# Strided attention and a SoLU layer on one core: a rebuilt first stage, and the mean taken off the activations instead of the weights

## The chip, the cores and the metric

The kernel runs on one core of one Trainium2 chip. The core has five engines with their own in-order instruction streams: TensorE (PE), VectorE (DVE), ScalarE (ACT), GpSimd (POOL) and SyncE (SP, which here only issues DMAs). The metric is the device time of one execution in microseconds; the figure shown is the median of three runs.

## What is computed

Eight batches, eight heads, 576 positions, head width 64. Four heads attend locally (the last 32 positions), four attend to every position with the same residue modulo 32. The 4608 x 512 result goes through a feed-forward layer with a softmax-weighted linear unit and a layer norm:

```python
scores = scale * np.matmul(q, k.transpose(0, 1, 3, 2))
mask_local = (rel >= 0) & (rel < 32)
mask_strided = (rel >= 0) & (pos[None, :] % 32 == pos[:, None] % 32)
attn = softmax(where(mask, scores, -1e9)); x = attn @ v      # to (4608, 512)
h = x @ w_in                                                  # 512 x 1024
sm = np.exp(h - h_max) / (np.sum(np.exp(h - h_max)) + 1e-09)
solu = h * sm
ln = (solu - mean(solu)) / np.sqrt(var(solu) + 1e-06) * g_ln
out = ln @ w_out                                              # 1024 x 512
```

q, k, v are float32. w_in and w_out come as 64-bit floats, 4 MB each, and are turned into float32 on the chip from their two 32-bit words. Products are kept near float32 by splitting each factor into a float16 part (hi) and a float16 remainder (lo) and adding three products.

## The kernel before

Every instruction group is a step with an engine, an estimated duration and a key (`Plan.add`). `Plan.order` walks a small model of the engines and emits the steps in the order in which the model would start them, the lowest key first among those that are ready. The order on each engine is therefore fixed when the program is written out; what the model gets wrong shows as waiting.

Attention runs in 40 units, five per batch (`UNITS`): two strided ones (54 queries x 54 keys in 6 and 5 blocks per head pair), then three local ones (64 x 96, 3 blocks). In `unit`, PE writes mask plus scores to `s_ps` (L347, L352), DVE takes the maximum and subtracts it (L358, L359), ACT takes the exp (L361), DVE the sums and reciprocals (L362, L366, L367), POOL multiplies (L370), ACT writes the hi part (L376) and DVE the lo part (L377) of p, a DMA transposes p to pt (L379), PE multiplies with v to `x_ps` (L400), and ACT and DVE write xhi and xlo (L416, L417) into a ring that the feed-forward part reads.

Per batch, `v_scale` squares v on ACT (L289), sums over partitions by f32 matmuls with a matrix of ones (`pow2_scale`, L254) and makes a power-of-two scale; `v_split` makes v's hi and lo parts (L307, L308). For the strided heads, two blocks of v lie in the two halves of the partitions, and four SBUF-to-SBUF DMAs a batch (L323) copy them to `vd`, so that one product takes p's hi and lo parts stacked in the partitions.

The feed-forward part has 36 tiles of 128 tokens (`ff`). G1: 24 matmuls of 512 columns to `h_ps` (L458 to L460). Then DVE's maximum (L465, L466), ACT's exp (L467), DVE's u = h times e with its sum (L469), the mean (L472), ACT's sum of (u - mean) squared (L473), POOL's norm (L477 to L487), c = u times r as hi on ACT (L490) and lo on DVE (L491), a DMA transpose to ct (L494). G2: 24 matmuls with w_out to `o_ps` (L498 to L500), and ACT scales and stores (L506, L507).

The weights are prepared once. `decode` reads a 512-column piece (L522), ACT widens one word (L525), DVE shifts and ors the other (L528, L529). `prep_w` squares w_in on ACT (L541), makes its scale, writes whi on ACT (L549) and gets wlo as a product on PE (L553, L555) that ACT copies (L557). `prep_o` does the same for w_out, and centres it: u's mean is not subtracted from u, but the weighted column mean is subtracted from w_out, with `gmat` (L567, L574) for the means and `split_o`'s `gdiag` and `ones` times `mt` (L590, L591) on PE, from which ACT and DVE write ohi and olo (L594, L595). Tile 0's G2 needs all of it.

Loads go out on SP in the order of the plan; SP waits when too many are outstanding.

Of the kernel before, what the change touches and what calls it, by code (L numbers as in the profile page):

```python
# [7 lines left out]
F32 = mybir.dt.float32  # L8
# [44 lines left out]
VK = [-25.0, *(5.0 * b - 8.0 for b in range(1, B))]  # L53
# [3 lines left out]
LF = [-62, -61, -59.55, -59.5, -59.45]  # L57
LW = [-60.0 + 0.1 * i for i in range(8)] + [-48.0 + 0.1 * i for i in range(8)]


class Plan:
# [12 lines left out]
    def add(self, eng, dur, fn, key, r=(), w=(), lock=None):  # L74
        n = len(self.steps)
        deps = set()
# [13 lines left out]
        self.steps.append((eng, dur, fn, key, deps, lock))  # L90

    def order(self):
# [15 lines left out]
        while len(out) < len(steps):  # L108
# [12 lines left out]
            if e == "sp":  # L121
                dma_free = max(dma_free, now + 0.55) + dur
                free[e] = max(now + 0.55, dma_free - self.DMA_AHEAD)
                end = dma_free + self.DMA_LATENCY
            else:
                if steps[n][5]:
                    now = max(now, locked["pool" if e == "dve" else "dve"])
                    locked[e] = now + dur
                free[e] = end = now + dur
# [10 lines left out]
def attn_solu_kernel(ctx: ExitStack, tc: tile.TileContext, qloc, qstr, kloc, kstr, vloc, vstr, w_in, w_out, g, masks, out):  # L140
# [13 lines left out]
    rooms = buf("room", [P, 1024], I32, n=4)  # L154
    (junk,) = buf("junk", [P, 6 * 4 * D], BF16)

    vr_sb = buf("vrl", [P, NCL * 4 * D]) + buf("vrs", [P, 6 * 4 * D])
    v_sb = buf("vl", [P, 2, NCL * 4 * D], F16) + buf("vs", [P, 2, 6 * 4 * D], F16)
    (ve_sb,) = buf("ve", [KL, 2, NCL * 4 * D], F16)

    (vd_sb,) = buf("vd", [P, 2, 6, 2, 4 * D], F16)
    vm_sb = buf("vm", [P, 4], n=2)
    vsc_sb = buf("vsc", [P, 5], n=4)
# [12 lines left out]
    e_sb = buf("e", [P, DF], n=2)  # L176
    u_sb = buf("u", [P, DF], n=2)
# [3 lines left out]
    st_sb = buf("st", [P, 16], n=4)  # L181
    (gmat,) = buf("gmat", [P, 8, P])
    (gdiag,) = buf("gdiag", [P, 8, P])
    (minus,) = buf("minus", [P, P], F16)
    (mt_sb,) = buf("mt", [P, DM])
    (nhalf,) = buf("nhalf", [P, 1])
    (ones,) = buf("ones", [P, P])
    (w16,) = buf("w16", [P, 4, 2, DF], F16)

    (obuf,) = buf("obuf", [P, 8, DM])  # L190
    o16 = obuf.bitcast(F16).rearrange("p c (a f) -> p c a f", a=2)
    whi, wlo = w16[:, :, 0, :], w16[:, :, 1, :]
    ohi, olo = o16[:, :, 0, :], o16[:, :, 1, :]
    (w_sc,) = buf("w_sc", [P, 8])
    (o_sc,) = buf("o_sc", [P, 16])
    (g_sb,) = buf("g", [P, 8])

# [8 lines left out]
    def init():  # L206
        nc.vector.memset(nhalf, -0.5)

    add("dve", 0.2, init, -9, w=["nhalf"])
# [9 lines left out]
    def load_masks(key):  # L219
        add("sp", 0.6, lambda: nc.sync.dma_start(mask_sb, masks), key, w=["mask_raw"])  # L220
        add("dve", 1.5, masks_bf16, key, r=["mask_raw"], w=["mask"])
# [8 lines left out]

    add("pool", 1.6, lambda: nc.gpsimd.memset(vd_sb[D:P, 1].bitcast(F32), 0.0), -9, w=["vz"])
# [14 lines left out]
    def pow2_scale(dst, parts, key, r, w, room, top=14, mul=1.0, square=None):  # L246
# [5 lines left out]
        def total():  # L252
            for i, part in enumerate(parts):
                nc.tensor.matmul(tot, ones, part, start=(i == 0), stop=(i == len(parts) - 1))  # L254

        add("pe", 0.2 * len(parts), total, key, r=["ones", *r], w=[T])
# [5 lines left out]
        def fn():  # L262
# [4 lines left out]
            if square:  # L267
                nc.vector.tensor_scalar(dst[:, 2:3], dst[:, 1:2], dst[:, 1:2], square, op0=ALU.mult, op1=ALU.mult)

        add("dve", 0.2, root, key, r=[T], w=[(w, "root")])  # L270
        add("dve", 0.5, fn, key, r=[(w, "root")], w=[w])


    def load_qk(b, half, key):
        w = 2 * (S, SP)[half]
        k0 = 0 if half else KPAD
        add("sp", 1.65, lambda: nc.sync.dma_start(q_raw[half][:, 0:w], (qloc, qstr)[half][b]), key, w=[("q", half)])
# [416 lines left out]
```

## Time and profile before

| | us |
|---|---|
| median of three runs | 572.67 |
| lowest and highest run | 567.52, 572.97 |
| span of the profiled execution, first to last instruction | 566.9 |
| PE, DVE, ACT, POOL busy in it | 505.7, 355.9, 301.8, 156.7 |

The profile gives no time of its own for the profiled execution beyond its span; that span is 0.6 us below the lowest run. Matmuls overlap on PE, so the sum of their durations in a group is more than the time that they took; the start-to-start distance is what counts. In a row of a group, "busy, mean ns" is followed by the idle time of the engine just before those instructions and by what ended it. In a row of the waits stand the total, the number of times and the longest. In a table of stretches each engine has its busy time and number of instructions, then come TensorE's granted clock (1.00 is full), the mean busy share of the 16 DMA engines and what they moved in GB/s.

### The profile page before, as it was taken

How to read it: one execution, taken by the hardware profiler on the slowest of the kernel's cores; microseconds unless marked ns; L12 is line 12 of the kernel's file. 1: busy time of each engine (PE TensorE's matmuls, PEld its weight loads, DVE VectorE, ACT ScalarE, POOL GpSimd, SP SyncE). 2: the span in 40 equal slices, each digit the busy share in tenths (PEclk: the TensorE clock that was granted, in tenths of full speed). 3: DMA queues.
4: the chain of work that ended last, by engine and by line, in shares of the span. 5: the costliest groups of instructions: out<-in, count | busy, mean ns of one | idle time of the engine just before them, and what ended most of it. 6: DMA issues, size and time to landing. Idle time of an engine off the chain costs nothing.

```text
span 566.9 us, 11879 instructions
## 1 busy us (share of the span) xinstructions
PE 505.7 (89%) x4864; PEld 256.9 (45%) x4864; DVE 355.9 (63%) x633; ACT 301.8 (53%) x446; POOL 156.7 (28%) x309
## 2 busy tenths in 40 slices
PE   0348998999798999899999999999989999999986
PEld 0233444345453555455454554555545554444432
DVE  3596367867466775677766776877656777343430
ACT  3765824685256553755674556555744644345350
POOL 2320002433132342334331332322323323113130
PEclk9999978899999999999999999999999999999999
DMA  8999149629992999599938996899679635533332
GB/s 312 413 258 272 35 120 227 140 59 247 190 250 56 225 217 237 127 175 236 254 86 122 271 221 138 198 206 240 162 137 180 139 80 111 87 84 84 77 91 74
DMA packets 171158, 96.90 MB, mean 171 GB/s; under 512 B 138208, under 2 KB 157280, under 8 KB 171104
## 3 DMA queue, kind: packets, MB, share of 16 engines
q1 hardware_dynamic: 165920, 86.71, 70.8%
q10 hardware_dynamic: 5184, 9.44, 5.1%
q8 instruction: 38, 0.62, 0.5%
q14 instruction: 16, 0.13, 0.1%
HBM read 39.24 MB, written 9.44 MB: 86 GB/s over the span
## 4 chain that ended last, share of the span: by engine, by line
PE 72%; DVE 10%; DMA 9%; ACT 5%; issue 2%; POOL 1%; ACTq 0%; SPq 0%; DVEq 0%
PE h_ps L458 10%; PE h_ps L459 9%; PE h_ps L460 9%; PE o_ps L498 9%; PE o_ps L499 9%; PE o_ps L500 9%; PE x_ps L400 4%; PE s_ps L352 4%; DMA pt<-p 3%; DMA ct<-c 2%; DVE u L469 2%; DMA vrl<-vloc 2%; ACT e L467 2%; PE h_ps L553 2%; PE s_ps L347 1%
## 5 line engine op out<-in xcount | busy, mean ns | idle before, releaser
L458 PE MATMUL h_ps<-w,xhi 128*128 128x512 f16 x280 | 108.5, 388 | 10.5 <-DVE u L469 7.6
L459 PE MATMUL h_ps<-w,xhi 128*128 128x512 f16 x280 | 108.2, 386 | 0.0
L460 PE MATMUL h_ps<-w,xlo 128*128 128x512 f16 x280 | 107.7, 385 | 0.0
L498 PE MATMUL o_ps<-obuf,ct 128*128 128x512 f16 x272 | 103.4, 380 | 1.0 <-DMA ct<-c 0.8
L499 PE MATMUL o_ps<-obuf,ct 128*128 128x512 f16 x272 | 103.3, 380 | 0.0
L500 PE MATMUL o_ps<-obuf,ct 128*128 128x512 f16 x272 | 103.2, 379 | 0.0
L370 POOL TENSOR_TENSOR t<-t,m 128x576 f32<-128x576 f32 (+2 forms) x40 | 47.4, 1184 | 126.9 <-DVE m L367 101.1
L467 ACT ACTIVATE e<-h_ps,st,vsc 128x1024 f32<-128x1024 f32 x31 | 37.2, 1201 | 64.8 <-DVE st L466 49.4
L465 DVE TENSOR_REDUCE st<-h_ps 128x1 f32<-128x1024 f32 x35 | 42.6, 1218 | 41.9 <-PE h_ps L460 41.9
L477 POOL TENSOR_SCALAR st<-st 128x1 f32<-128x1 f32 x36 | 11.4, 316 | 208.3 <-DVE st L472 198.8
L469 DVE SCALAR_TENSOR_TENSOR u<-h_ps,e 128x1024 f32<-128x1024 f32 x35 | 42.8, 1222 | 29.1 <-ACT e L467 17.7
L473 ACT ACTIVATE e<-u,st 128x1024 f32<-128x1024 f32 x36 | 41.3, 1147 | 35.3 <-DVE st L472 32.1
L491 DVE SCALAR_TENSOR_TENSOR c<-u,st,c 128x1024 f16<-128x1024 f32 x36 | 47.0, 1304 | 14.6 <-ACT c L490 14.6
L417 DVE TENSOR_TENSOR xlo<-x_ps,xhi 128x384 f16<-128x384 f32 (+2 forms) x40 | 25.6, 641 | 40.4 <-ACT xhi L416 40.3
L490 ACT ACTIVATE c<-u,st 128x1024 f16<-128x1024 f32 x36 | 41.2, 1145 | 16.8 <-POOL st L487 16.0
L459 PEld LDWEIGHTS <-xhi 128*128 128x128 f16 x288 | 28.5, 99 | 40.2 <-issue 12.9
L498 PEld LDWEIGHTS <-ct 128*128 128x128 f16 x288 | 28.2, 98 | 39.4 <-DMA ct<-c 5.5
L458 PEld LDWEIGHTS <-xhi 128*128 128x128 f16 x288 | 28.8, 100 | 35.4 <-issue 5.9
L460 PEld LDWEIGHTS <-xlo 128*128 128x128 f16 x288 | 28.6, 99 | 35.4 <-issue 2.5
L500 PEld LDWEIGHTS <-ct 128*128 128x128 f16 x288 | 28.2, 98 | 34.2 <-issue 0.3
L499 PEld LDWEIGHTS <-ct 128*128 128x128 f16 x288 | 28.2, 98 | 32.3
L352 PE MATMUL s_ps<-k,q 64*54 64x54 f32 (+1 forms) x1280 | 41.8, 274 | 0.0
(143 smaller groups left out, 766.2 us busy)
## 6 DMA issues: line engine op xcount, KB each, us to landing
out<-ob ACTq DMA_DIRECT2D x36, 256.0 KB, 3.1
vrs<-vstr SPq DMA_DIRECT2D x8, 768.0 KB, 5.8
vd<-vs SPq DMA_DIRECT2D x16, 384.0 KB, 7.5
vrl<-vloc SPq DMA_DIRECT2D x8, 640.0 KB, 5.7
q<-qstr SPq DMA_DIRECT2D x8, 594.0 KB, 4.9
k<-kstr SPq DMA_DIRECT2D x8, 594.0 KB, 6.5
q<-qloc SPq DMA_DIRECT2D x8, 576.0 KB, 5.2
k<-kloc SPq DMA_DIRECT2D x8, 576.0 KB, 6.8
```

Of the source, the lines that this page charges most:

```text
L352: nc.tensor.matmul(s_ps[row : row + nq, pair, i * nk : (i + 1) * nk], q_raw[half][hs, q0 : q0 + (nq - 1) * nqb + 1 : nqb], k_raw[half][hs, ...
L370: add("pool", nx * nk / 500 + 0.1, lambda: nc.gpsimd.tensor_tensor(tv, tv, sm.unsqueeze(2).broadcast_to([P, nx, nk]), op=ALU.mult), key + ...
L458: nc.tensor.matmul(hv[:, i], xhi[:, cc, tok], whi[:, cc, cols], start=(cc == 0), stop=False)
L459: nc.tensor.matmul(hv[:, i], xhi[:, cc, tok], wlo[:, cc, cols], start=False, stop=False)
L460: nc.tensor.matmul(hv[:, i], xlo[:, cc, tok], whi[:, cc, cols], start=False, stop=(cc == 3))
L465: add("dve", 1.21, lambda: nc.vector.tensor_reduce(nm, hv, axis=AX.XY, op=ALU.max, negate=True), key + 0.2, r=HH, w=[(ST, "nm")])
L467: add("act", 1.3, lambda: nc.scalar.activation(ev, hv, AF.Exp, bias=nm, scale=hs, accum_out=z), key + 0.25, r=[*HH, (ST, "nm"), *SC], w=[E ...
L469: add("dve", 1.3, lambda: nc.vector.scalar_tensor_tensor(uv, hv, 1.0, ev, op0=ALU.mult, op1=ALU.mult, accum_out=us), key + 0.3, r=[*HH, E] ...
L491: add("dve", 1.35, lambda: nc.vector.scalar_tensor_tensor(c[:, 1], u, r, c[:, 0], op0=ALU.mult, op1=ALU.subtract), key + 0.45, r=[U, (ST, ...
L498: nc.tensor.matmul(o, ct[:, cc, :], ohi[:, cc, :], start=(cc == 0), stop=False)
L499: nc.tensor.matmul(o, ct[:, cc, :], olo[:, cc, :], start=False, stop=False)
L500: nc.tensor.matmul(o, ct[:, 8 + cc, :], ohi[:, cc, :], start=False, stop=(cc == 7))
```

## The change

- **Strided v.** `vd` and its four copies a batch are gone. `load_v` reads the strided v twice from HBM, once to partitions 0 to 63 and once to 64 to 127, in two transfers of 64 partitions; `vrs` and `vs` are twice as wide (3072 columns), and the split covers both places. The products read `vs` where they read `vd`.
- **Sums of squares.** For w_in and for batch 0's v, PE forms the Gram matrix of the upper 16 bits of the floats, and one DVE pass sums its diagonal. For later batches ACT squares in three passes instead of two. `pow2_scale` sums the parts on DVE and over partitions with one bf16 matmul.
- **Decoding** works on 1024 columns a piece: four pieces of 1 MB for each weight. w_in's lo part is made on PE for two row blocks as before, on DVE for the other two.
- **The mean** is subtracted from u: c = (u - mean), hi on ACT as an activation with a bias, lo on DVE; r is left to the store's factor f. u is scaled by a power of two `ia` made from the row's largest value. The squares come after c, and POOL's five small passes make f from them. w_out is scaled by g and a power of two, with no product on PE.
- **lo of p** goes to POOL for batch 0's units (`POOL_LO`).
- **Order.** `Plan.ahead` gives every step that the first tile's G1, and then its G2, depends on a key by its longest chain. The planner's model of DMAs counts outstanding pushes; durations are changed throughout. w_out's loads are held in the plan until the transposes of units 1 and 2 are issued, later loads until certain transposes.

```diff
+    def ahead(self, target, base):
+        tail = {target: 0.0}
+        for n in range(target, -1, -1):
+            if n not in tail:
+                continue
+            for d in self.steps[n][4]:
+                tail[d] = max(tail.get(d, 0.0), tail[n] + self.steps[n][1] + self.HOP)
+        for n, t in tail.items():
+            s = list(self.steps[n])
+            lands = s[6][2] + s[6][3] if s[6] else 0.0
+            s[3] = min(s[3], base - t - s[1] - lands)
...
+    def gram(dst, pieces, key, w, room, scrap):
+        acc, A = room
+        for i, (x, r) in enumerate(pieces):
+            def products(i=i, x=x):
+                y = x.bitcast(BF16).rearrange("p (f t) -> p f t", t=2)
+                n = x.shape[1]
+                for f in range(0, n, P):
+                    z = y[:, f : f + P, 1]
+                    nc.tensor.matmul(acc, z, z, start=(i == 0 and f == 0), stop=(i == len(pieces) - 1 and f == n - P))
...
+        add("dve", 0.35, lambda: nc.vector.scalar_tensor_tensor(scrap, acc, 2.0 ** (-2 * SQ), unit_sb, op0=ALU.mult, op1=ALU.mult, accum_out=dst),
...
+        add("pe", 0.15, lambda: nc.tensor.matmul(tot, ones, one, start=True, stop=True), key, r=["ones", *r], w=[T])
...
+        for i in range(2):
+            def twice(i=i):
+                nc.sync.dma_start(vr_sb[1][i * D : i * D + D].rearrange("p (y f) -> p y f", y=2), vstr[b].rearrange("(y p) f -> p y f", y=2))
...
-            moves = [(1.5, vd_sb[0:D, :, :, y], vn[y * D : y * D + D]) for y in range(2)]
-            moves += [(0.8, vd_sb[D:P, 0, :, y], vn[y * D : y * D + D, 0]) for y in range(2)]
+            moves = ()
...
+        if b < POOL_LO:
+            add("pool", nx * nk / 510 + 0.02, lambda: nc.gpsimd.tensor_tensor(lo, tv, hi, op=ALU.subtract), key + 0.45, r=[T, PB], w=[PB])
...
+        add("dve", 0.2, lambda: nc.vector.tensor_tensor(st[:, 0:3], low.broadcast_to([P, 3]), sc[:, 0:3], op=ALU.mult), key + 0.2,
...
+        def span():
+            nc.vector.tensor_scalar(near, up, floor, down, op0=ALU.max, op1=ALU.max)
+            nc.vector.tensor_scalar(ia.bitcast(I32), near.bitcast(I32), 0x7FFFFFFF, 0x7F800000, op0=ALU.bitwise_xor, op1=ALU.bitwise_and)
...
-        add("act", 1.2, lambda: nc.scalar.mul(c[:, 0], u, r), key + 0.4, r=[U, (ST, "r")], w=[(C, 0)])
+        add("act", 1.2, lambda: nc.scalar.activation(c[:, 0], u, AF.Identity, bias=mean, scale=1.0), key + 0.35, r=[U, (ST, "mean")], w=[(C, 0)])
+        add("dve", 1.28, lambda: nc.vector.scalar_tensor_tensor(c[:, 1], u, mean, c[:, 0], op0=ALU.add, op1=ALU.subtract), key + 0.4,
+        add("act", 1.24, lambda: nc.scalar.activation(junk[:, 0:DF], u, AF.Square, bias=mean, scale=1.0, accum_out=sq), key + 0.42,
...
-                nc.tensor.matmul(x, gdiag[:, cc], obuf[:, cc], start=True, stop=False)
-                nc.tensor.matmul(x, ones[0:1], mt_sb[0:1], start=False, stop=True)
+            add("act", 0.68, lambda cc=cc, go=go: nc.scalar.mul(ohi[:, cc], o32[:, cc], go), key, r=[("od", cc), "go"], w=[("oh", cc), *past])
+                add("dve", 0.7, lambda cc=cc, go=go: nc.vector.scalar_tensor_tensor(olo[:, cc], o32[:, cc], go, ohi[:, cc], op0=ALU.mult, op1=ALU.subtract), key,
...
+    for target, base in ((second[1], -200.0), (second[0], -200.0), (first[1], -400.0), (first[0], -400.0)):
+        plan.ahead(target, base)
```

More of the change, by code (lines that the diff above doesn't have):

```diff
@@ new lines, in v_scale, with square @@
+        parts = () if b == 0 else ((vr_sb[0], 0), (vr_sb[1][:, 0 : 6 * 4 * D], 1), (vr_sb[1][:, 6 * 4 * D :], 1))
+        for i, (x, a) in enumerate(parts):
+            def square(i=i, x=x):
+                nc.scalar.activation(junk[:, 0 : x.shape[1]], x, AF.Square, scale=2.0**-SQ, accum_out=vm[:, i : i + 1])
+            add("act", (1.36, 1.58)[a], square, key, r=VR[a], w=["junk", ("vm", b % 2, i)])
+        pow2_scale(sc, vm[:, 0 : 3 if b else 1], vs1_sb[b % 2], key, [("vm", b % 2, i) for i in range(3 if b else 1)], ("vsc", b % 4),
+                   (o_ps[:, P : P + 1], "o") if b == 0 else (s_ps[:, 1, 511:512], ("s", 1)), 8, 1.0 / P_SCALE)
@@ L303, in v_split @@
+        add("dve", 0.36, hscale, key + 0.5, r=[("vsc", b % 4), "w_sc", "consts"], w=[("hsc", b % 4)])
     def v_split(b, a, key):
@@ L557, in prep_w @@
+                add("pe", 1.4, rest, key, r=["wdiag", "minus", ("wh", cc), *ST[cc]], w=[X])
                 add("act", 0.62, lambda cc=cc, x=x, cols=cols: nc.scalar.copy(wlo[:, cc, cols], x), key, r=[X], w=[("w", cc, i)])
     def prep_o(key):
-        for cc in range(8):
-            decode(obuf[:, cc], w_out[cc * P : (cc + 1) * P, :], key, ("od", cc), O_ROOMS[cc], 8 + cc)
-            add("act", 0.6, lambda cc=cc: nc.scalar.activation(ob_sb[cc % 2][:, 0 : DM // 2].bitcast(BF16), obuf[:, cc], AF.Square,
-                                                               scale=2.0**-SQ, accum_out=o_sc[:, 8 + cc : 9 + cc]), key,
-                r=[("od", cc)], w=[("om", cc), ("ob", cc % 2)])
@@ L566, in gains @@
-        def gains():
-            nc.gpsimd.tensor_scalar(gmat, g_sb.unsqueeze(2).broadcast_to([P, 8, P]), -1.0 / DF, None, op0=ALU.mult)
-        add("pool", 2.3, gains, key - 5, r=["g"], w=["gmat"])
-        add("pool", 2.3, lambda: nc.gpsimd.tensor_tensor(gdiag, unit_sb.unsqueeze(1).broadcast_to([P, 8, P]), g_sb.unsqueeze(2).broadcast_to([P, 8, P]), op=ALU.mult),
-            key - 5, r=["g", "unit"], w=["gdiag"])
-        for cc in range(8):
-            add("pe", 0.87, lambda cc=cc: nc.tensor.matmul(o_ps, gmat[:, cc], obuf[:, cc], start=(cc == 0), stop=(cc == 7)), key,
-                r=["gmat", ("od", cc)], w=["o"])
@@ L577, in comb @@
[L577 to L583 removed]
+        add("pool", 0.3, lambda: nc.gpsimd.tensor_tensor(gg_sb[:, 0], g_sb, g_sb, op=ALU.mult), key, r=["g"], w=["gg"])
@@ new lines, in prep_o @@
+        for i in range(4):
+            dst, D2 = o32[:, 2 * i : 2 * i + 2], [("od", 2 * i), ("od", 2 * i + 1)]
+            decode(dst, w_out[2 * i * P : (2 * i + 2) * P].rearrange("(c p) (f t) -> p c f t", c=2, t=2), key, D2, ROOMS[(i + 2) % 4], 4 + i, [turned[AFTER_O[i]]])
+            for cc in (2 * i, 2 * i + 1):
+                add("act", 0.8, lambda cc=cc: nc.scalar.activation(ob_sb[cc % 2][:, 0 : DM // 2].bitcast(BF16), o32[:, cc], AF.Square,
+                                                                   scale=2.0**-SQ, accum_out=o_sc[:, 4 + cc : 5 + cc]), key,
+                    r=[("od", cc)], w=[("om", cc), ("ob", cc % 2)])
```

335 lines of the change are left out of this document (181 added, 154 removed).

## The prediction

> **What bounds the kernel now.** I read the page first (span, busy shares, 40 slices), then a table of stretches, the timeline of PE, PE's waits, and the chain of waits at the end.
>
> ```profile
> span 566.9 us, 11879 instructions
> ...
> core 0: us, PE busy (x) PEld busy (x) DVE busy (x) ACT busy (x) POOL busy (x), PEclk, DMA share, GB/s
> 0.00:10.00 10.00, 0.00 (x0) 0.00 (x0) 1.67 (x8) 1.88 (x2) 4.07 (x15) 1.00 0.80 272
> 10.00:20.00 10.00, 0.30 (x2) 0.30 (x2) 5.24 (x10) 6.42 (x12) 0.00 (x0) 1.00 1.02 414
> 0.00:66.40 66.40, 30.26 (x328) 17.48 (x329) 39.13 (x78) 41.59 (x71) 13.38 (x21) 1.00 0.92 275
> 66.40:123.30 56.90, 53.21 (x401) 24.45 (x399) 38.95 (x76) 29.07 (x45) 13.79 (x24) 0.88 0.59 135
> 100.00:540.00 440.00, 424.16 (x4176) 215.51 (x4171) 289.83 (x501) 240.52 (x347) 134.88 (x271) 0.99 0.78 163
> ```
>
> From 100 to 540 us PE is busy 424.16 of 440: that stretch is bound by PE, and 15.8 us of waits are all that any other engine could give there. What is slack lies in front. Until 66.4 us PE works 30.26 and idles 36.1; and of the 53.21 that it works from 66.4 to 123.3, part is preparation. The timeline of PE names the milestones:
>
> ```profile
> 19.70 0.58 PE L254 MATMUL s_ps<-vm,ones 128*128 128x1 f32 x2 [19.70 <-ACT junk L289]
> 22.65 0.49 PE L347 MATMUL s_ps<-mk_str,unit 64*64 64x324 bf16 x4 [0.75 <-DVE vsc L260]
> 66.47 0.38 PE L458 MATMUL h_ps<-w,xhi 128*128 128x512 f16 x1
> 66.69 0.38 PE L459 MATMUL h_ps<-w,xhi 128*128 128x512 f16 x1
> 123.32 0.39 PE L498 MATMUL o_ps<-obuf,ct 128*128 128x512 f16 x1
> ```
>
> The scores of unit 0 (L347) need only q, k and the masks, and the masks were there at 6.7 us (below); they start at 22.65 because PE, in order, first waits for ACT's squares of v. The first product for a token tile ("G1", L458) starts at 66.47, the first output product ("G2", L498) at 123.32. Two matmuls of 512 columns in a row start 0.22 us apart (66.47, 66.69), whatever their modelled 0.38.
>
> **What the change takes from PE.** Centring w_out on PE (gmat and mt, then gdiag plus ones times mt) goes; the mean now leaves u directly.
>
> ```profile
> L591 PE MATMUL x_ps<-mt,ones 1*128 1x512 f32 x16 | 9.9, 702 | 0.0
> L590 PE MATMUL x_ps<-obuf,gdiag 128*128 128x512 f32 x16 | 8.6, 617 | 0.8 <-DVE obuf L595 0.8
> L254 PE MATMUL h_ps<-o_sc,ones 128*128 128x1 f32 x16 | 1.9, 251 | 0.0
> L254 PE MATMUL s_ps<-vm,ones 128*128 128x1 f32 x32 | 5.0, 255 | 20.7 <-ACT junk L289 20.7
> ```
>
> The first three lie behind 66.4 us, where PE has nearly no idle time: 9.9 + 8.6 + 1.9 = 20.4 us of path, all gone (w_out's sum becomes one small bf16 matmul). The sums of v's squares (5.0 us for 8 batches; the busy times overlap) become one bf16 pass each instead of four f32 ones: I take 2 us, bounds 0 and 3.5. The gmat products, half of the w_in residual products and w_in's sum lie ahead of 66.4 and are counted in the next step. Grams are added on PE: 32 matmuls of 128 columns for w_in, 34 for v. A 128x1 matmul costs at most 0.255 us and a 512-column one starts 0.22 after the last, so a piece costs 2 to 3 us, in a stretch where PE idles 36.1: no cost of its own beyond the tail below.
>
> The granted clock in 66.4 to 123.3 was 0.88, that is 0.12 x 56.9 = 6.8 us lost. With fewer waits and fewer one-column passes I take 2 us back, between 0 and 5.
>
> **When the first G1 starts.** Three lower bounds, then a choice.
>
> ```profile
> 6.73 0.21 DVE L214 CAST mk_loc<-mask 128x96 bf16<-128x96 f32 x1 [5.61 <-DMA mask<-masks]
> 14.80 0.42 DVE L528 TENSOR_SCALAR room<-room 128x512 int32<-128x512 int32 x1
> 26.03 1.53 DVE L528 TENSOR_SCALAR room<-room 128x512 int32<-128x512 int32 x1
> 27.66 0.69 DVE L529 SCALAR_TENSOR_TENSOR ct<-ct,room 128x512 int32<-128x512 int32 x1
> 28.27 1.81 DVE L308 SCALAR_TENSOR_TENSOR vs<-vrs,vsc,vs 128x1536 f16<-128x1536 f32 x1
> 31.44 1.27 POOL L370 TENSOR_TENSOR t<-t,m 128x648 f32<-128x648 f32 x1 [4.17 <-DVE m L367]
> 34.34 0.82 DVE L377 TENSOR_TENSOR p<-t,p 128x648 f16<-128x648 f32 x1
> 40.41 1.15 ACT L549 ACTIVATE w<-c,w_sc 128x1024 f16<-128x1024 f32 x1 [2.26 <-DVE w_sc L264]
> 40.41 0.92 DVE L547 TENSOR_SCALAR mt<-unit,w_sc 128x128 f32<-128x128 bf16 x1
> 48.81 0.58 ACT L557 CAST w<-h_ps 128x512 f16<-128x512 f32 x1
> ```
>
> (1) Data. The first G1 needs q, k, both v and all of w_in: by their shapes 8.97 MB, v's strided half counted twice. The first 10 us moved 2.72 MB, after that 414 GB/s: all landed at 10 + 6.25/0.414 = 25.1 us. w_out's loads, until now in between, are placed on SP behind the transposes of units 1 and 2. (2) The tail behind the last piece of w_in: decode on ACT 1.3 and DVE 1.1 (0.42 + 0.69; twice as wide now, but the shift can run ahead), its Gram 0.5 to 2, diagonal, sum and scale 1.2, four hi parts at 1.15 = 4.6, four residual copies at 0.58 = 2.3, one DVE residual 1.3 (by the 1.24 of u, a DVE pass of 1024 columns below), and ten hand-overs of 0.1 to 0.2: 14. So 39. (3) DVE. It was busy 39.13 until 66.4. Off: all of w_out's decoding, 8 x (0.42 + 0.69) = 8.9; unit 3, some 3.4 (four passes of 0.73, the 0.82 row at 576 of 648 columns, and two small ones); three lo parts that move to POOL, 2.3; wdiag 0.92, also to POOL. On: the strided v split is twice as wide, +1.8; two w_in residuals, 2.6; two diagonals of Grams, 0.7. Leaves 28.7, and it can start at 6.73: 35.4 if it never waits. Each lo on POOL costs about its row's 1.27 against 0.82, 0.5 us a unit on the chain. A DVE pass beside a POOL one can be held (1.53 instead of 0.42 at 26.03, while POOL ran): at most three times 1.1. POOL itself was busy 13.38 of the 66.4, so three more passes find room there.
>
> DVE used 65% of the time from 6.7 to 66.4 (39.13/59.7); at that share 28.7 would take 44 and end at 51. I take **43**: nearer the data bound, since the largest single wait, unit 0 behind the squares, goes, and the four vd copies that stood ahead of the first strided PV go with their SP issues and landings. Gain 66.5 - 43 = 23.5; bounds 38 and 51.
>
> **Between the first G1 and the first G2.** G2 needs w_out, and one whole trip of tile 0. The last tile shows that trip:
>
> ```profile
> 543.77 1.24 DVE st L465
> ...
> 546.67 1.24 DVE u L469 x2
> ...
> 547.93 0.17 DVE st L472
> ...
> 550.95 1.16 ACT c L490
> ...
> 553.48 4.24 DMA ct<-c
> ```
>
> Now c follows the mean at once: 550.95 - 548.10 = 2.85 us of square and norm leave the chain (they run beside the transpose and G2; the store is what waits for them). At the end of the kernel nothing covers this, so it counts whole: 2.7 us after a hand-over. Tile 0 takes 5.2 of G1 (24 x 0.22) and then 553.48 + 4.24 - 543.77 - 2.85 = 11, so G2 comes at 60 at the earliest. Until then PE has G1 of tiles 0 to 3 (20.8) and units 3 and 4, but DVE must do w_out's decoding (8.9) and residuals (8 of half a u, 5), units 3 and 4 (about 7.7 less a POOL lo each) and two tiles' passes (9): 30 us, of which perhaps 8 fit in its gaps before 43. So DVE is done near 65, and PE idles some 8 us in that time, against 56.9 - 53.2 = 3.7 in the old stretch: a net cost of 4, between 0 and 10. Unit 2's and 3's scores, done before 66.4 in the old order, partly come later: 1.
>
> **The steady part.** Per tile DVE gains two passes over a few columns beside the exp (0.36, two like the mean's 0.17), per batch the wider split 1.8; ACT per batch one more pass over v and a wider split, about 3. All of it beside a PE that is busy 96%: 8 x 1.8 + 36 x 0.36 = 27 us if it all stood in front of PE, nothing if hidden. This row decides:
>
> ```profile
> PE h_ps L458 <- DVE u L469: 7.6, 8, 2.7
> ```
>
> PE waited for DVE's u 7.6 us in eight of 36 tiles, with DVE at 66% (289.83/440). A shorter chain speaks for less, more passes for more: 0, bounds -6 and +8. Of the DMAs, the vd copies (1152 KB a batch) go and 768 KB of a second load come; loads wait on SP until the transposes ahead of them are issued. 0 as well.
>
> **The sum.** 566.9 - 23.5 (start) - 20.4 (centring) - 2 (v's sums) - 2 (clock) - 2.7 (end) + 4 + 1 = 521.3. The three runs were 567.52 to 572.97: the lowest stands 0.6 above the span, the median 5.8. I add 3.2, the middle: about **525**, against 572.67.
>
> **The rivals.**
> Thin feed: in-order DVE meets the new order badly, first G1 at 51 and G2 ten us later than the tile allows. For it: DVE's 65% of before. Price 8 + 6 + 2 more: 541. Chance 0.18.
> Half-rate halves: the strided v arrives in two transfers of 64 partitions. vd copies of that width took longer than wider loads:
>
> ```profile
> vrs<-vstr SPq DMA_DIRECT2D x8, 768.0 KB, 5.8
> vd<-vs SPq DMA_DIRECT2D x16, 384.0 KB, 7.5
> ```
>
> At 414 GB/s each takes 1.9 us, at half of it 3.8: 3.8 more for the first stage's data, and 3.8 a batch later where the DMA share is 0.78 on average. Price 4 at the start, little after: 529. Chance 0.13. [...]
> Better: first G1 at 39, no gap, and the steady waits fall by 6 with the shorter chain: 525 - 4 - 4 - 6 - 3 = 508. Chance 0.13.
> Slower: c's hi part is now an activation with a bias (Identity) where a plain scaling stood. If that function needed another table, ACT would reload twice a tile.
>
> ```profile
> L525 ACT ACT_TABLE_LOAD x1 | 1.3, 1283 | 0.8 <-PEq L684 0.8
> ```
>
> 36 x 2 x 1.283 = 92 us on ACT; with all of it in front of PE 617. It decides against the change when over half of it, 48 us, is exposed. Against it: one load served Prelu, Square, Exp and the scaling. Chance 0.03. [...]
> No change: DVE's 27 us all in front of PE and the first G1 not before 60: 525 + 27 + 17 = 569. Chance 0.03.
>
> **How the numbers follow.** The forecast itself (512 to 535) has 0.50, the rest as above. The range 508 to 545 leaves out half of the better case, some of the thin feed, and the last two: about 0.18. A measurement here can tell about 1% from no change. Faster by over 1% (below 567): 0.94; within it 0.03; slower 0.03.
>
> **What would show it.** In the new profile: the first L458-like matmul on h_ps between 38 and 51; scores of unit 0 before 10 us; no f32 matmul of w_out; first G2 at 60 to 70; one table load; from the last u to its c under 0.6 us; PE's waits for u at or below 8 us. The forecast is wrong if the first G1 stays behind 51, if PE idles more than 12 us before the first G2, or if PE's busy share between 100 us and the end falls below 94%.

## The result: 7% slower, and the profile after

| | before | after |
|---|---|---|
| median of four runs, us | 570.2 | 611.55 |
| lowest and highest, us | 567.52, 572.97 | 604.52, 613.72 |
| span of the profiled execution, us | 566.9 | 609.0 |

The ratio is 1.069 (95% interval 1.059 to 1.079); it leaves out the run of 613.72 us, which lies over 1.5% above the fastest one. The forecast was 525, with 508 to 545 as its range: the time moved the other way. The profiled run of the changed kernel took 610.75 us.

The page of the changed kernel, first busy time and instructions, then the span in 40 slices (each digit a busy share in tenths, the last row the granted clock):

```profile
PE 502.6 (83%) x4824; PEld 252.3 (41%) x4824; DVE 380.0 (62%) x687; ACT 312.4 (51%) x435; POOL 140.4 (23%) x252
...
PE   1655596885999689997999599997999699989996
...
DVE  2785678823697449844796449734895449844460
...
PEclk9765796997999989997999989998999889999999
```

PE starts its work early, as forecast, but behind slice 10 it has a dip every few slices. DVE alternates between 3 to 4 and 8 to 9 tenths; before, its steady part stood mostly at 6 and 7. The same in stretches:

```profile
0.00:100.00 100.00, 57.45 (x614) 32.15 (x614) 65.53 (x115) 54.76 (x77) 25.41 (x47) 0.76 0.75 212
100.00:540.00 440.00, 385.01 (x3848) 192.74 (x3850) 287.76 (x526) 230.93 (x320) 103.86 (x176) 0.95 0.72 153
```

Between 100 and 540 us PE idles 440 - 385.0 = 55.0 us, where it idled 440 - 424.2 = 15.8 before. These 39 us are most of the loss of 42.1 in span. The centring left PE, 26.0 us by its three groups (9.9, 8.6 and gmat's 7.5), and the Grams came, 8.1 us by theirs. Yet PE's busy time fell only from 505.7 to 502.6: the matmuls that stayed ran longer, at a granted clock of 0.76 in the first 100 us and 0.95 from 100 to 540 (before: 0.95 and 0.99). What PE waited for in the whole run:

```profile
PE h_ps L532 <- DVE eu L554: 30.6, 10, 4.2
PE s_ps L417 <- DVE t L429: 8.9, 13, 4.0
PE h_ps L532 <- ACT xhi L490: 7.2, 5, 4.3
...
PE o_ps L297 <- DMA vrs<-vstr: 5.9, 1, 5.9
```

G1 (L532) waits for the u of the tile ahead (L554): the row that was 7.6 us is now 30.6. Single rows of PE's timeline show the marks that the prediction named, the scores of unit 0, the Gram of the strided v, w_in's residual on PE, the first G1 and the first G2:

```profile
7.41 1.51 PE L422 MATMUL s_ps<-k,q 64*54 64x54 f32 x48 [2.78 <-DMA k<-kstr]
14.81 2.72 PE L297 MATMUL o_ps<-vrs 128*128 128x128 bf16 x24 [5.90 <-DMA vrs<-vstr]
...
41.80 2.07 PE L632 MATMUL h_ps<-c,wdiag 128*128 128x512 f32 x2 [1.81 <-POOL wdiag L619]
...
58.17 0.61 PE L532 MATMUL h_ps<-w,xhi 128*128 128x512 f16 x1 [4.28 <-ACT xhi L490]
...
83.53 0.38 PE L577 MATMUL o_ps<-obuf,ct 128*128 128x512 f16 x1
```

So the first G1 is 8 us earlier than before and the first G2 40 us; the start was won and more than lost behind it. One batch of the steady part, in windows of 10 us, first the changed kernel:

```profile
200.00:210.00 10.00, 7.49 (x67) 3.76 (x67) 4.51 (x10) 4.18 (x7) 1.42 (x4) 1.00 1.07 230
210.00:220.00 10.00, 5.77 (x21) 2.16 (x20) 3.45 (x8) 7.02 (x10) 0.80 (x3) 0.83 0.45 92
230.00:240.00 10.00, 9.49 (x127) 5.51 (x126) 9.75 (x14) 6.41 (x8) 2.65 (x4) 1.00 0.97 190
240.00:250.00 10.00, 8.63 (x119) 4.97 (x119) 9.90 (x19) 7.20 (x12) 5.20 (x6) 1.00 0.61 126
```

then the kernel before:

```profile
200.00:210.00 10.00, 10.00 (x140) 5.76 (x133) 8.28 (x14) 5.53 (x9) 3.10 (x6) 1.00 1.27 217
210.00:220.00 10.00, 10.00 (x80) 4.72 (x79) 6.02 (x9) 5.86 (x8) 4.86 (x8) 1.00 1.13 217
```

DVE alone does not make the difference: the kernel before has one such full slice too (9.69 of 10 from 240 to 250). In the changed kernel the strided q and k and both v of the next batch go out together, here in SP's queue between 193 and 197 us, and one wait of G1 shows what follows:

```profile
193.15 0.89 SPq L338 DMA_DIRECT2D q<-qstr  x1
194.09 0.43 SPq L339 DMA_DIRECT2D k<-kstr  x1
194.56 1.47 SPq L351 DMA_DIRECT2D vrs<-vstr  x2
196.08 0.68 SPq L346 DMA_DIRECT2D vrl<-vloc  x1
```

```profile
212.66 0.16 DVE L541 TENSOR_TENSOR st<-st,vsc 128x3 f32<-128x3 f32 x1
...
212.91 1.20 ACT L551 ACTIVATE eu<-h_ps,st,vsc 128x1024 f32<-128x1024 f32 x1 [4.10 <-DVE st L541]
...
214.24 1.28 DVE L554 SCALAR_TENSOR_TENSOR eu<-h_ps,st,eu 128x1024 f32<-128x1024 f32 x1 [0.93 <-ACT eu L551]
...
215.59 0.59 PE L532 MATMUL h_ps<-w,xhi 128*128 128x512 f16 x1 [4.23 <-DVE eu L554]
```

The local v landed 14.2 us after its issue, at 210.3, and ACT squares it from 214.1 on. Between 188 and 227.7 us PE's timeline has no scores of any unit, only tiles and the last products of the units before, and tiles alone feed PE badly: G1 needs a bank of h_ps that the tile ahead frees with its u, 4.23 us after that tile's G1 ended (largest value, exp, u: three passes that hand over to each other). This wait came six times between 100 and 540 us with the same 4.23 us, 66 to 74 us apart, which is about once a batch. The units of the batch then run in a bunch, with DVE at 9.8 of 10.

### The profile page after: what moved, and what is told of

The parts are those of the page before. It is cut to its first block, busy times and chain, and to the rows that moved or that the text cites. A ratio compares the mean times of both kernels' runs of the same rounds, so it can differ in the third digit from the quotient of the medians.

```text
span 609.0 us, 11792 instructions
## 1 busy us (share of the span) xinstructions
PE 502.6 (83%) x4824; PEld 252.3 (41%) x4824; DVE 380.0 (62%) x687; ACT 312.4 (51%) x435; POOL 140.4 (23%) x252
## 4 chain that ended last, share of the span: by engine, by line
PE 51%; DVE 26%; DMA 9%; ACT 7%; issue 5%; POOL 1%; SPq 0%; ACTq 0%; DVEq 0%; POOLq 0%
PE h_ps L532 10%; PE h_ps L534 10%; PE h_ps L533 9%; PE o_ps L577 5%; DVE eu L554 5%; PE o_ps L578 5%; PE o_ps L579 5%; DMA ct<-c 5%; DVE st L540 4%; DVE vs L378 4%; ACT vs L377 3%; PE x_ps L474 3%; DMA g<-g 3%; DVE m L428 2%; DVE m L432 2%
## 5 line engine op out<-in xcount | busy, mean ns | idle before, releaser
L532 PE MATMUL h_ps<-w,xhi 128*128 128x512 f16 x280 | 113.3, 405 | 41.6 <-DVE eu L554 30.6
L534 PE MATMUL h_ps<-w,xlo 128*128 128x512 f16 x280 | 113.3, 405 | 2.9 <-DVE xlo L491 1.7
L533 PE MATMUL h_ps<-w,xhi 128*128 128x512 f16 x280 | 113.1, 404 | 0.0
L554 DVE SCALAR_TENSOR_TENSOR eu<-h_ps,st,eu 128x1024 f32<-128x1024 f32 x35 | 44.8, 1281 | 57.8 <-ACT eu L551 39.4
L551 ACT ACTIVATE eu<-h_ps,st,vsc 128x1024 f32<-128x1024 f32 x31 | 37.3, 1204 | 64.0 <-DVE st L541 35.6
L559 DVE SCALAR_TENSOR_TENSOR c<-eu,st,c 128x1024 f16<-128x1024 f32 x36 | 49.2, 1368 | 32.4 <-ACT c L558 32.1
L567 POOL TENSOR_SCALAR st<-st 128x1 f32<-128x1 f32 x36 | 20.1, 559 | 188.4 <-ACT junk L561 187.7
L558 ACT ACTIVATE c<-eu,st 128x1024 f16<-128x1024 f32 x36 | 41.2, 1144 | 42.1 <-DVE st L557 40.4
L431 ACT ACTIVATE t<-t 128x576 f32<-128x576 f32 (+2 forms) x40 | 27.5, 688 | 47.7 <-DVE t L429 44.3
L532 PEld LDWEIGHTS <-xhi 128*128 128x128 f16 x288 | 29.3, 102 | 50.4 <-ACT xhi L490 15.2
L565 POOL TENSOR_SCALAR st<-st 128x1 f32<-128x1 f32 x36 | 15.7, 436 | 131.2 <-ACT eu L551 116.2
L578 PEld LDWEIGHTS <-ct 128*128 128x128 f16 x288 | 28.6, 99 | 38.8 <-issue 10.9
L577 PEld LDWEIGHTS <-ct 128*128 128x128 f16 x288 | 28.5, 99 | 38.4 <-DMA ct<-c 5.0
L446 ACT CAST p<-t 128x576 f16<-128x576 f32 (+2 forms) x40 | 27.0, 675 | 33.7 <-POOL t L440 33.6
## 6 DMA issues: line engine op xcount, KB each, us to landing
vrs<-vstr SPq DMA_DIRECT2D x16, 768.0 KB, 11.5
```

The lines of the kernel that those rows point to most:

```text
L532: nc.tensor.matmul(hv[:, i], xhi[:, cc, tok], whi[:, cc, cols], start=(cc == 0), stop=False)
L533: nc.tensor.matmul(hv[:, i], xhi[:, cc, tok], wlo[:, cc, cols], start=False, stop=False)
L534: nc.tensor.matmul(hv[:, i], xlo[:, cc, tok], whi[:, cc, cols], start=False, stop=(cc == 3))
L554: add("dve", 1.3, lambda: nc.vector.scalar_tensor_tensor(uv, hv, ia, ev, op0=ALU.mult, op1=ALU.mult, accum_out=us), key + 0.3, r=[*HH, E, ...
L558: add("act", 1.2, lambda: nc.scalar.activation(c[:, 0], u, AF.Identity, bias=mean, scale=1.0), key + 0.35, r=[U, (ST, "mean")], w=[(C, 0)])
L559: add("dve", 1.28, lambda: nc.vector.scalar_tensor_tensor(c[:, 1], u, mean, c[:, 0], op0=ALU.add, op1=ALU.subtract), key + 0.4, r=[U, (ST, ...
```

## The experiments

Each was run with the kernel before beside it; its medians there were 568.4 to 571.0. The first four change one thing in the changed kernel. Theory A: the strided v's transfers of 64 partitions run at half rate. B: the plan holds the loads back too long. C: the split of v, twice as wide and in one piece, holds the units.

**e1**: v laid out twice in HBM, two transfers of 128 partitions.

```diff
-nc.sync.dma_start(vr_sb[1][i * D : i * D + D]..., vstr[b]...)
+nc.sync.dma_start(vr_sb[1][:, i * 6 * 4 * D : (i + 1) * 6 * 4 * D], vstr[b][:, i * 6 * 4 * D : (i + 1) * 6 * 4 * D])
```

> Strided v reaches the same two places by two transfers of 128 partitions and 768 KB each (its source laid out twice in HBM), instead of two of 64 partitions; the order of every engine stays as it is in the changed kernel. Theory A (64-partition transfers run at half rate and everything planned behind them comes late): v lands in some 6 us instead of 11.5, the first G1 starts near 48 instead of 58, PE's waits between 100 and 540 us fall from 55 to below 25, and the time to 535 to 560. Theory B (the loads are issued too late, behind the transposes that the plan names): time above 590. Theory C (the split of v, 2.84 us on ACT and 3.42 on DVE in one piece, is what holds the units): time above 590.

Measured: 603.15 us (1.057; 1.051 to 1.063), first G1 at 52.2, waits for u 30.9, as in the changed kernel. Rows of the DMA issues, first the changed kernel, then e1:

```profile
vrs<-vstr SPq DMA_DIRECT2D x16, 768.0 KB, 11.5
```

```profile
vrs<-vstr SPq DMA_DIRECT2D x16, 768.0 KB, 8.2
```

The same bytes in the same order land 3.3 us sooner at 128 partitions. The narrow transfers cost 8 us by the medians, 7 by the ratios, and they cost it at the start: the first G1 is 6.0 us earlier, and the waits for u behind it stay. Theory A's 535 to 560 is missed.

**e2**: the plan is told 3.9 us for each half.

```diff
-            add("sp", 1.95, twice, key, w=[("vr", 1, i)], dma=LOAD, after=after)
+            add("sp", 3.9, twice, key, w=[("vr", 1, i)], dma=LOAD, after=after)
```

> The changed kernel with one number of the planner different: each half load of the strided v is planned at 3.9 us instead of 1.95. The transfers stay as they are, the order of the engines follows the new number. Theory A, if the harm is mainly that a wrong duration makes a wrong order: 560 to 585. Theory A, if the harm is the lateness itself, whatever the order: 595 to 615. Theories B and C: 600 to 615, no change.

Measured: 632.67 us (1.109; 1.103 to 1.114). This is outside all three expectations: planning the loads longer made a worse order.

**e3**: no holding back of the loads of batches 1 to 7.

```diff
-            load_qk(b, 1, LK[b], [turned[b * NU - 3]])
+            load_qk(b, 1, LK[b])
```

> The changed kernel without the wait in the plan that puts the loads of batches 1 to 7 behind certain transposes; w_out's loads stay behind theirs. Theory B: v and q, k of the next batch come 10 us and more earlier, units spread between the tiles again, PE's waits between 100 and 540 us fall from 55 to below 25, time 550 to 575. Theory A: a transfer that starts earlier hides some of its length in the later batches, 585 to 605, the first G1 unchanged at 58. Theory C: no change, 600 to 615.

Measured: 584.78 us (1.026; 1.020 to 1.032), 27 us under the changed kernel. G1 waits 9.3 us for u in the whole run, where it waited 30.6:

```profile
L532 PE MATMUL h_ps<-w,xhi 128*128 128x512 f16 x280 | 112.5, 402 | 16.8 <-DVE eu L554 9.3
```

DVE is still bunched (9.69, 9.79, 8.78 of 10 between 210 and 240 us), yet PE is busy 10.00, 10.00 and 8.52 there. The edit changes two things at once, the loads' time and the order: DVE's instructions stand in another order than in the changed kernel, so the 27 us are not split between the two.

**e4**: strided v loaded once, split at half the width, four copies as before.

```diff
-        for i in range(2):
-            add("sp", 1.95, twice, key, w=[("vr", 1, i)], dma=LOAD, after=after)
+        add("sp", 1.95, lambda: nc.sync.dma_start(vr_sb[1], vstr[b]), key, w=[("vr", 1)], dma=LOAD, after=after)
...
-            moves = ()
+            moves = [(2.1, 48, vd_sb[0:D, :, :, y], vn[y * D : y * D + D]) for y in range(2)]
+            moves += [(1.1, 24, vd_sb[D:P, 0, :, y], vn[y * D : y * D + D, 0]) for y in range(2)]
```

> The changed kernel with the strided v as before: loaded once (768 KB over 128 partitions), split at half the width, and copied by four transfers in SBUF to the second place. All else as in the changed kernel. Theory A: 540 to 570, the copies cost some of what the loads give. Theory B: above 590. Theory C: 545 to 575, and lower than with the 128-partition loads.

Measured: 583.8 us (1.024; 1.018 to 1.030), first G1 at 46.3.

**e5**: e3 and e4 together.

> The changed kernel with two undoings at once: the strided v is loaded once and copied apart as before, and the loads of later batches wait for nothing but their turn on SP. Each alone gave about 27 us (584.8 and 583.8 against 611.5). If the late loads and the double v are two separate costs, both come off: 611.5 - 27 - 28 = 556, below the kernel before. If they are one cost, the late v that makes the five units run bunched, the two overlap: 575 to 582, DVE still at 9 or more in 10 us for some stretches of every batch, PE busy 402 to 408 of the 440 us from 100 to 540.

Measured: 575.54 us (1.009; 1.005 to 1.013). The two overlap. With both undone the time is still not below the kernel before, though the first G1 comes at 48.7 and PE is busy 15.7 us less (490.0). The loss is not in a single transfer, so the next runs start from the kernel before.

**e6**: the kernel before, with only the mean taken off the data (the feed-forward chain and w_out's preparation of the change; nothing else).

```diff
-        add("act", 1.2, lambda: nc.scalar.mul(c[:, 0], u, r), key + 0.4, r=[U, (ST, "r")], w=[(C, 0)])
+        add("act", 1.2, lambda: nc.scalar.activation(c[:, 0], u, AF.Identity, bias=mean, scale=1.0), key + 0.35, r=[U, (ST, "mean")], w=[(C, 0)])
...
-            add("pe", 1.8, center, key, r=["gdiag", "ones", "mt", ("od", cc)], w=[X])
```

> The kernel before with only the mean taken off the data: w_out is no longer centred by products on TensorE, the hi part c is the activation with the mean as bias, the spread's norm follows beside the transposes; first stage, loads, v's copies, keys and planner as before. By the prediction's terms: 569.4 - 20.4 (centring) - 2.7 (end), so 546, if the steady part keeps its cover (PE busy 420 or more of 440 us, waits for u under 10 us). If the new feed-forward chain itself is what lets the tiles wait for u (two more DVE passes ahead of exp, square on ACT after c), the waits for u grow to 25 us or more here too and the time stays at 565 to 580.

Measured: 620.25 us (1.091; 1.084 to 1.097), slower than the whole change. PE is busy 505.9 us as before, though the centring is gone, and idles 50 us between 100 and 540; its largest waits there are for the transposes of c (18.2 us) and for xlo (12.8), not for u (8.1):

```profile
100.00:540.00 440.00, 389.97 (x3852) 196.26 (x3851) 276.94 (x510) 213.45 (x308) 99.96 (x177) 0.93 0.75 154
```

**e7**: the kernel before, strided v in two transfers of 64 partitions.

```diff
+            for i in range(2):
+                nc.sync.dma_start(vr_sb[1][i * D : i * D + D], vstr[b][i * D : i * D + D])
```

> The kernel before with one edit: the strided v comes in two transfers of 64 partitions, 384 KB each, in place of one of 768 KB. Half rate for 64 partitions: each half takes about as long as the whole did, the median from issue to landing goes from 5.8 us to 8 or more, the first strided PV moves by 2 to 4 us, and the whole by 0 to 6 us: 569 to 575. Full rate: landing stays near 6 and the time within 2 us.

Measured: 575.5 us (1.011; 1.007 to 1.015), some 6 to 7 us more. Row of the DMA issues:

```profile
vrs<-vstr SPq DMA_DIRECT2D x16, 384.0 KB, 7.7
```

A half of 384 KB landed 7.7 us after its issue (median), where the whole of 768 KB took 5.8. The two halves stand one behind the other in SP's queue (the first two at 4.91 us, 1.88 us of issuing together) and the median is over both, so this row alone does not show a rate; the two rows of e1 compare the same bytes in the same order, 11.5 and 8.2 us.

**e8**: e5 with the planner's model of the kernel before.

```diff
-                end = dma_free + lands + (LATE0 if steps[n][6] == LOAD and now < 20 else self.LATE)
+                end = dma_free + self.DMA_LATENCY
...
-                free[e] = end - (0.16 if dur > 2.4 else self.SKIP[e])
+                free[e] = end = now + dur
```

> The kernel of e5 (v once, loads not gated) with the order worked out by the costs and rules of the kernel before: a load costs 5 us after its transfer, engines are free when a pass ends, no queue depth. If the new costs of the plan are what bunches the units, DVE's work per 10 us is even again (5 to 8 in every slice), PE is busy 415 or more of 440 us and the time is 12 us or more under that of e5. If the order follows from the keys and the chains, it stays within 6 us of e5.

Measured: 580.97 us (1.021; 1.015 to 1.027), within 6 us of e5, with DVE at 9.0, 9.1 and 9.6 of 10 between 200 and 230 us: the new costs in the plan are not what bunches the units.

What was left was the order itself. `Plan.order` picks greedily among ready steps, so that an edit of a step or of its cost can draw a new order for everything behind it.

**e9**: e6's arithmetic, each step at the place that the kernel before gives it. The plan gets the steps, costs and keys of the kernel before; a step fills the place of the one that it replaces, and places without a step stay empty. The squares go to the tile's own buffer instead of the shared scrap.

```diff
-        add("act", 1.35, ...Square..., key + 0.35, r=[U, (ST, "mean")], w=[E, (ST, "sq")])
+        add("act", 1.35, lambda: nc.scalar.activation(c[:, 0], u, AF.Identity, bias=mean, scale=1.0), key + 0.35, r=[U, (ST, "mean")], w=[E, (ST, "sq")])
...
-            add("pe", 1.8, center, key, r=["gdiag", "ones", "mt", ("od", cc)], w=[X])
+            add("pe", 1.8, nothing, key, r=["gdiag", "ones", "mt", ("od", cc)], w=[X])
```

> The arithmetic of e6 (mean off the data, no centring of w_out on TensorE) with every step at the place that the kernel before gives it: the plan is worked out with the steps, costs and keys of the kernel before, and the steps that went are left empty. If it is the order that cost e6 its time, and not the new chain of a tile, PE's busy time in 100 to 540 us is 420 or more of 440, waits for u under 10 us, and the time is 569 - 20 (centring) - 0 to 3 = 546 to 549. If the chain itself is too long for the tiles (two passes more ahead of exp, no chain on GpSimd), the waits for u stay and the time is 570 to 615.

Measured: 566.91 us (0.992; 0.987 to 0.996). This lies between the two numbers expected: the order is worth 53 us between e6 and e9 (the squares' place apart; in e6 only ACT writes the scrap, so it makes no other engine wait), but of the 20 us of centring only 3 came. The first G2 comes at 113.2, 10 us earlier than in the kernel before, and from there to the end it takes 451.9 us instead of 443.6.

**e10**: the kernel before, one number of its plan changed by 0.01 us.

```diff
-        add("act", 1.3, lambda: nc.scalar.activation(ev, hv, AF.Exp, ...
+        add("act", 1.29, lambda: nc.scalar.activation(ev, hv, AF.Exp, ...
```

> The kernel before, the same instructions, with one number of its plan changed: the exp is planned at 1.29 us in place of 1.30. The plan then places 98 of PE's 266 steps, 226 of DVE's 506 and 67 of SP's 198 differently. If the order of the kernel before is one good draw among many, this costs 10 to 40 us (579 to 610), with DVE's work bunched and waits for u, c or v. If neighbouring orders are alike, the time stays within 4 us of 569.

Measured: 581.64 us (1.021; 1.015 to 1.027). The same instructions, 12 us slower.

**e11**: the kernel before, the plan told that a centring step takes 0.05 us.

```diff
-            add("pe", 1.8, center, key, r=["gdiag", "ones", "mt", ("od", cc)], w=[X])
+            add("pe", 0.05, center, key, r=["gdiag", "ones", "mt", ("od", cc)], w=[X])
```

> The kernel before, the same instructions (centring included), with the plan told that each centring step takes 0.05 us on TensorE in place of 0.87 and 1.8. Its real work is that of the kernel before, so an order as good as before gives 569 to 573. If the loss of e6 came with the order that follows from taking the centring out of the plan, this one loses too: 590 or more.

Measured: 586.57 us (1.030; 1.027 to 1.032): 17 us for an order drawn as if PE had this time free.

**e12**: e5 with two kinds of key. Steps that the kernel before places ahead of its first G2 keep the place that the new plan gives them; all others follow in the order of the kernel before.

```diff
-    for n in plan.order():
+    for n in plan.merged():
...
+        key = [(0, pos[n]) if rank[n] is None else (1, rank[n]) for n in range(len(self.steps))]
```

> The kernel of e5 (the change, with v once and loads not gated), but all steps that the kernel before places from its first G2 on (123.3 us there) stand in the order of the kernel before, behind all others, which keep the new plan's order; the spread's square is written to the tile's own buffer. If the loss is the order of the steady part: PE is busy 415 or more of 440 us, the first G2 comes near 100, about 20 us before that of the kernel before, and the time is 545 to 555. If the new first stage gains nothing, or the tiles' longer chain of passes does not fit the old order, 565 to 580.

Measured: 553.11 us (0.970; 0.963 to 0.976), 16 us faster than the kernel before and 22 faster than e5. The first G2 comes at 106.3, 17 us earlier than in the kernel before; from there to the end both take the same time (443.3 and 443.6 us). This is the best version found.

**e13**: the same with the strided v as in the change. Against the changed kernel the order differs, with the loads at their old places and no longer held back, and the squares go to the tile's own buffer.

> As e12, with the strided v as in the change: loaded to both places by two transfers of 64 partitions, the split twice as wide, no copies. If the double v costs only its own passes (ACT 1.4 and DVE 1.7 more per batch, split in one piece), the time is 0 to 8 us over e12. If the split in one piece and the later landing hold the units in this order too, 15 us or more over e12.

Measured: 578.85 us (1.014; 1.006 to 1.023). That is 33 us under the changed kernel and 26 over e12. Of the 33, 27 are there in e3 already, which has the same work and loads that are not held back; the old order adds 6, which is little beyond the noise. The steady part of both, e12 first:

```profile
100.00:540.00 440.00, 420.37 (x4106) 211.88 (x4106) 293.35 (x551) 232.81 (x337) 126.05 (x201) 0.99 0.77 160
```

```profile
100.00:540.00 440.00, 406.50 (x4022) 204.67 (x4015) 301.84 (x549) 243.79 (x342) 130.91 (x195) 0.98 0.71 152
```

**e14**: e12, with the square and the split of the strided v done a second time into scrap, from batch 1 on.

```diff
+            if a and b:
+                nc.scalar.mul(junk[:, 0:w], vr_sb[a], sc[:, 1:2])
```

> The kernel of e12 with the passes of the double v added where they stand in the change, from batch 1 on: the square, the hi part and the lo part of the strided v are each done a second time (into scrap), at the same place; loads and copies stay those of e12. If the 26 us are the passes (per batch 3.2 us more of ACT, 1.8 of DVE, in one go ahead of the units), this gives 565 to 575. If they are the late landing, the wide piece's wait for it and the buffer that the next split must wait for, it stays at 553 to 560.

Measured: 566.45 us (0.992; 0.989 to 0.995): with the passes alone 13 of the 26 us are there. In the profiled runs e13 takes 25.7 us more than e12: 8.7 ahead of the first G2 (at 115.0 against 106.3) and 17.0 behind it. Of these 17.0 the passes of e14 give 12.8 (456.1 us from the first G2 to the end against 443.3); 4 stay unexplained.

**e15**: e13 with the split in two pieces of 1536 columns.

```diff
+        for i in range(pieces):
+            p = slice(i * w // pieces, (i + 1) * w // pieces)
+            add("act", w / pieces / 1140 + 0.24, lambda p=p: nc.scalar.mul(hi[:, p], vr_sb[a][:, p], sc[:, 1:2]), key, ...
```

> The kernel of e13 with the split of the strided v in two pieces of 1536 columns, the second at the places where the kernel before issued its copies. If the one wide piece (2.84 us of ACT, then 3.42 of DVE) held the units and tiles behind it, half or more of the 26 us go: 553 to 566. If it is the number of passes or the first stage's late landing, the time stays at 572 to 582.

Measured: 581.19 us (1.017; 1.010 to 1.023), no better. The start was drawn anew too (first G1 at 61.7 instead of 56.2), so this run speaks against the one wide piece but does not price it.

**e16, e17**: e12 with the G2s of the first two, or four, tiles also in the first part.

```diff
+            if tag in ('ff0', 'ff1'):
+                out.append(None)
+                continue
```

> The kernel of e12 with all steps of tiles 0 and 1 in the new plan's part, so that their G2s (4 halves of 2.6 to 2.75 us, 10.5 us of TensorE) stand in the first 100 us in place of after 106. If TensorE's idle time there is free to take them, the first G2 comes near 75 to 85 and the time falls by 5 to 10 us: 543 to 548. If DVE sets the pace there and behind, TensorE only idles later instead: 551 to 556.

> The same with tiles 0 to 3 (21 us of TensorE ahead). If the idle time takes them: 536 to 545. If the G2s in a row hold back the strided halves of attention that stand behind them in TensorE's queue, or DVE sets the pace: 551 to 565.

Measured: 556.8 us (0.977; 0.971 to 0.984) and 564.05 us (0.987; 0.978 to 0.995). The first G2 came at 73.8 and 74.1, over 30 us earlier than in e12, and the time did not fall: e16 is the same as e12 within their intervals, e17 is slower.

## Why the prediction failed, step by step

From the changed kernel's 611.6 us the old order with freed loads takes 33 (e13), and v loaded once takes another 26 (e12). What is left of the change then stands 16 us under the kernel before.

**The steady part** (forecast 0, between -6 and +8; measured: 39 us more idle PE). This is the step that failed most. The row that decided it, PE's 7.6 us of waiting for u, was taken for a property of the tile's chain. It is a property of the order in which the engines get their steps: over the whole run it is 30.6 in the changed kernel, and with the same chain and the same passes 9.3 in e3 and 18.3 in e13; in e12 it is 12.2. The prediction costed every part as a shift inside a fixed order, while the planner drew a new one; e10 shows what that can be worth with no change of work at all. The second term at 0 in the same step was that the loads wait for transposes: without that wait the time is 27 us less (e3). Whether the loads' lateness or the order drawn with it makes these 27 is not shown. Order and held loads together cost 33 us (e13 against the changed kernel). In the profiled runs 502.6 - 488.0 = 14.6 of them are slower matmuls: e13 has the same 4824 and is busy 488.0 us. The parts do not add: with v twice, freeing the loads gives 27 us and the old order behind it 6; with v once, 8 (e5 against e4) and 22 (e12 against e5).

**The double v** (forecast 0 for the transfers, 0 for the wider passes as hidden work; measured: 26 us with the old steady order kept). The sizes of the passes were right, about 3 us of ACT and 1.8 of DVE a batch; that they are hidden beside a busy PE was not. Half of the loss (13) came with such passes alone: in e14 ACT is busy 2.9 us and DVE 1.7 us more in each of seven batches than in e12, and these passes stand ahead of the tiles' passes in the same queues. The rival of half-rate halves was right in direction and priced at 4; the narrow transfers cost 7 to 8 in e1 and 6 to 7 in e7. The half rate from which its 4 was worked out was a supposition that no run shows: the same bytes landed in 11.5 us at 64 partitions and in 8.2 at 128.

**The first G1** (forecast 43, between 38 and 51; measured 58.2). PE's Gram of v waited 5.9 us for the transfer's end at 14.8 and stood ahead of unit 1's scores in PE's queue; w_in's residuals on PE ran in f32 at half the clock (granted 0.50 from 41 to 53 us), 2.07 us a pair. The landing of v, taken at the 414 GB/s that the kernel before moved from 10 to 20 us, is one mis-sized term: with 128 partitions the first G1 comes at 52.2 (e1), 6.0 us earlier and still outside the bounds. With v once it is 46.3 (e4) to 49.5 (e12), inside them, so the double bytes and the wider passes were the other. The prediction's own count by DVE's share gave 51; it took 43, and the start gave 8.3 us instead of 23.5.

**The centring** (forecast -20.4) and **the start** (forecast -23.5) were added, and that sum was wrong in itself. Where the steady order is kept, both together give 16 (e12), the centring alone 3 (e9). The stretch from the first G1 to the first G2, e12 first and then the kernel before:

```profile
49.45:106.31 56.86, 37.53 (x350) 18.34 (x351) 48.38 (x87) 36.54 (x59) 11.64 (x18) 0.74 0.80 197
```

```profile
66.47:123.32 56.85, 53.16 (x401) 24.46 (x400) 38.95 (x76) 29.02 (x45) 13.81 (x24) 0.88 0.59 135
```

It has the same length, though PE is busy 15.6 us less in it. PE was busy 94% there before and looked like the bound, but DVE needs its time for the same stretch: with w_out's work moved into it DVE is busy 48.4 of 56.9 us. The chain that ended last runs over DVE for at least 27.0 of the 56.9 us in e12 and for 10.2 before; 9.1 us of the 27.0 are w_out's residuals (6.6) and one of the two passes of its decoding (2.5). PE's clock adds to it, granted at 0.74 instead of 0.88: behind a wait of 6.0 us (e12, at 101.6) G1's matmuls start 0.43 us apart in place of 0.22. The prediction had counted DVE's work ("30 us" between first G1 and first G2) and put its cost at 4. In the changed kernel itself that term came out: PE idles 7.3 us in a stretch of 25.4, where some 8 were forecast. e16 and e17 fit: more of PE's work ahead of 106 us does not shorten the whole.

**The end.** The chain is shorter as forecast; here its passes for the last tile, largest value, u and c's hi part:

```profile
585.14 1.22 DVE L540 TENSOR_REDUCE st<-x_ps 128x1 f32<-128x1024 f32 x1 [0.85 <-PE x_ps L534]
...
588.28 1.28 DVE L554 SCALAR_TENSOR_TENSOR eu<-x_ps,st,eu 128x1024 f32<-128x1024 f32 x1
...
589.79 1.15 ACT L558 ACTIVATE c<-eu,st 128x1024 f16<-128x1024 f32 x1 [1.26 <-DVE st L557]
```

c starts 0.2 us after u. From the largest value to the end of the span it was 609.0 - 585.1 = 23.9 us, against 566.9 - 543.8 = 23.1 before: G2s of earlier tiles stand on PE in front of it, so the 2.7 us did not come. The clock's -2 has the wrong sign: the granted clock fell from 0.95 to 0.76 in the first 100 us and from 0.99 to 0.95 from 100 to 540. The sums of v's squares fell from 5.0 us to 1.3, a little more than the 2 that were forecast.

**Right**: unit 0's scores at 7.4, no centring on PE, c 0.2 us after u, and one table load (1.28 us, at 0.78 us), with c's hi part as an activation with a bias. The first G2 came 40 us earlier, but at 83.5, not at 60 to 70. Of the marks against it, two came true: the first G1 behind 51, and PE's share from 100 us to the end, 87% (445.1/509.0), below 94%. The third did not, if it is taken from the first G1 on: PE idled 7.3 us there, not over 12. The thin feed was the only rival with a new order in it, and it counted that order in the first stage alone; none had a new order of the steady part, and a chance of 0.03 for "slower" was too small for that reason.

**Open**: how good an order for the whole change could be. Orders of nearly the same work gave 567 and 620 (e9, e6), 553 and 575 (e12, e5), 569, 582 and 587 (before, e10, e11). The held loads and the new keys are part of the change, what the planner draws from them is not; no run parts the 33 us between the two. What in an order is good or bad also stays open: e6 waits for other things than the changed kernel does.

## What to carry to other kernels

Where a planner or scheduler writes the order, first shake it (one cost by 0.01 us) and see how far the time moves; a change that is worth less than that can be judged only with the old order kept. Busy time taken from an engine that is 94% busy is a gain only if the next engine of that stretch has room for the work of the stretch; look at each engine's busy time between two fixed steps. Two gains that end at the same step cannot simply be added.

## What the runs showed of the hardware

A short pause of PE can cost more than its length. After one wait of 4.16 us in e6, PE's timeline (start, duration) goes on at half the rate:

```profile
239.62 0.61 PE L504 MATMUL o_ps<-obuf,ct 128*128 128x512 f16 x1 [4.16 <-DMA ct<-c]
240.02 0.63 PE L505 MATMUL o_ps<-obuf,ct 128*128 128x512 f16 x1
...
245.98 0.39 PE L504 MATMUL o_ps<-obuf,ct 128*128 128x512 f16 x1
246.21 0.38 PE L505 MATMUL o_ps<-obuf,ct 128*128 128x512 f16 x1
```

The starts are 0.43 us apart for some 5 us and 0.22 then, so the pause is followed by about 2.5 us more. In the changed kernel five of six pauses of 4.2 us between 100 and 540 us were followed at once by matmuls of 0.6 us; the sixth, before 350.5 us, was followed by them about 1 us later. Why the delay differs is not shown. The length alone does not decide whether the rate falls: after a pause of 2.46 us (e12, at 532.7) half rate was there as well, for 3 us, and after one of 2.71 us (e12, at 158.96) it was not.
